# Mamba-2 scan followed by a low-rank mixer: moving the w2 conversions and pair 5's scaling, lending y's banks to pair 3, and pacing the late loads

## The chip, the cores and the metric

One core of one Trainium2 chip runs the whole program. The metric is the device time of one execution in microseconds (us), and the median of several executions where a single number is given. The engines are named as in the profile: PE is the matrix engine (PEld its weight loads), DVE the vector engine, ACT the scalar engine, POOL the general engine, SP the engine that issues the DMAs.

## The reference

Two blocks run one after the other. The first is a chunked state-space scan over 4 batches, 8 heads, 768 positions, head size 32, state size 16, in chunks of 32. The second mixes the first one's output (4 x 768 x 256) along the sequence with a low-rank product and then applies two dense layers.

```
for each chunk c of 32 positions:
    L = exp(cum_i - cum_j) where i >= j, else 0        # cum = cumsum(log a)
    y = ((C B^T) * L) x + (C state) * exp(cum)
    state = exp(sum log a) * state + sum_j B_j x_j exp(cum_end - cum_j)
u  = y + (y^T U V)^T
out = u + relu(u w_ch1) w_ch2
```

U, V, w_ch1 and w_ch2 come as 64-bit floats and are converted to 32 bits on the chip.

## The kernel before, in words

The scan works on *pairs* of 128 positions: `pairs[k]` is batch k // 3 and the (k % 3)-th 256 positions, so there are 12 pairs, k = 0 to 11. "Pair 3" below is k = 3, the first pair of batch 1. Pair k passes these steps, each a function:

- `load_bc(k)` (L111) and `load_x(k)` (L121) issue four loads of B and C and two of x, on SP. All loads of all pairs and all weights stand at the head of SP's program; the stores of the output (L764) come behind them.
- `prep(k)` (L339) scales B and C of the pair by their decays, one DVE instruction (L344) into the tile BC. `decayed(k)` (L351) makes bd from B on POOL (L356).
- `turning(k)` / `turn(k)` (L363) transposes BC on PE into a PSUM bank (tag "w" unless told otherwise), and ACT copies it out: T (L378) and two masked copies Cm (L384).
- `gram(k)` (L398) computes C B^T into four PSUM banks: two of tag "x" and two of tag "z". `mask(k)` (L410) copies them to M with the causal mask, four DVE instructions (L417).
- `state(k)` (L429), on PE, makes each chunk's contribution to the state; `update(k)` (L444) runs the recurrence, three or four DVE instructions (L456, L458), and one POOL instruction (L465) writes Sm.
- `inter(k, 0)`, `intra(k)`, `inter(k, 1)` (L499, L528) are the matmuls of the output, in the two banks of tag "y"; `yout(k)` (L542) copies y out on ACT, and `ytokening(k)` (L551) transposes it back ("tokens").

The first matmul of `inter(k, 1)` waits for whatever instruction was put into `behind["part"]` since `inter(k, 0)`: in the main loop that is the first masking instruction of pair k + 1 on DVE. `apart(copy)` (L469) sets it to a tiny copy instead, which itself waits for the matmuls of `inter(k, 0)`.

There are eight PSUM banks, two for each of the tags w, x, z and y; a tag's banks are handed out in turn, and a bank comes free when its last reader is done.

`to_fp32` (L299) converts one block of 64-bit words in three steps, which other code pulls one at a time: step 1 is two DVE instructions (e, L315, and top, L317) and one on ACT (rest, L319); step 2 is one on ACT (power, L321); step 3 is three on DVE (L323, L325, L327). There are ten blocks in order: U and V together, two eighths and three quarters of w_ch1, and four blocks of w_ch2, called w2 a, b, c and d here. `convert(n)` (L865) runs the next n steps; `convert_ahead()` (L869) runs steps 1 and 2 of the *next* block and then step 3 of the current one.

The dense layers of batch 0 are run plainly. `up` (L701, relu L706 on ACT) fills the first layer in 8 column blocks, m = 0 to 7, each with an x bank and a z bank; `some(2)` runs one m. `down(0)` of batch 0 is two calls of `whole` (L806): two transposes (L810) and then all eight w2 row blocks in order (L816), the last two of which are block d. The other `down` groups (L741) use sums on DVE (L730) and the combined weights `w2s`, made by `operands` (L1010, instructions on L1013).

All engines run in the order in which the code emits (`manual_schedule`), and each engine's queue is strictly in that order. The order around the change is written out by hand: from `mixed()` of batch 0 on it is a list of calls, and from L1028 a loop over k = 3, 4, 5, ... that does prep(k+2), a piece of dense work (`plan`), turning(k+2), inter(k,0), gram(k+1), intra(k), state(k+1), mask(k+1), inter(k,1), yout(k), update(k+1). The `o` tiles that hold the output before its store exist three times.

Of the kernel before, what the change touches and what calls it, by code (L numbers as in the profile page):

```python
# [20 lines left out]
def kernel(  # L21
# [27 lines left out]
    nc = tc.nc  # L49
    P = 128  # L50
# [3 lines left out]
    NPR = NC // 2  # L54
# [8 lines left out]
    H = 64  # L63
# [30 lines left out]
    def fill(n):  # L94
# [10 lines left out]
        in_=a.rearrange("(g b) h (c s) -> g (b h c) s", g=2, s=P).rearrange(  # L105
            "g r s -> r g s"))

    x_sb, bc_sb = {}, {}
    pairs = [(b, q) for b in range(NB) for q in range(NPR)]

    def load_bc(k, blocks=(0, 1)):  # L111
        b, q = pairs[k]
        if k not in bc_sb:
            bc_sb[k] = raw.tile([P, 2, 2, NH, N], FP32, tag="bc", name="bc")
        for c in blocks:
            for i, src in enumerate((B, C)):
                nc.sync.dma_start(  # L117
                    out=bc_sb[k][:, i, c],
                    in_=src[b, :, ts(2 * q + c, P), :].rearrange("h s n -> s h n"))

    def load_x(k, blocks=(0, 1)):  # L121
        b, q = pairs[k]
        if k not in x_sb:
            x_sb[k] = raw.tile([P, 2, NH, D], FP32, tag="x", name="x")
        for c in blocks:
            nc.sync.dma_start(  # L126
                out=x_sb[k][:, c],
                in_=x[b, :, ts(2 * q + c, P), :].rearrange("h s d -> s h d"))


    UV = const.tile([P, 2, NC * RK], FP32)
# [24 lines left out]
    for k in range(NPR):  # L156
# [4 lines left out]
        if k:  # L161
# [4 lines left out]
                      in_=U2.rearrange("(c p) r -> p c r", p=P))  # L166
# [5 lines left out]
    for k in range(2):  # L172
# [3 lines left out]
                                      in_=w13[:, :, ts(k, 2 * P)]))  # L176
# [4 lines left out]
    for m in range(0, NM, 2):  # L181
        load_words(w2[:, m:m + 2],
                   w22[m * P:(m + 2) * P].rearrange("(m p) d -> p m d", p=P))
    for k in range(NPR + 1, NB * NPR):
        load_bc(k)
        load_x(k)


    ident = const.tile([P, P], FP32)
# [54 lines left out]
    for b in range(NB):  # L244
        g, o = divmod(b * NH * NC, R)
# [93 lines left out]
    def prep(k, c=0, n=2):  # L339

        b, q = pairs[k]
        if c == 0:
            st[k] = {"BC": att.tile([P, 2, 2, NH, N], FP32, tag="BC", name="BC")}
        nc.vector.tensor_tensor(  # L344
            out=st[k]["BC"][:, :, c:c + n].rearrange("p i c h n -> p i (c h) n"),
            in0=bc_sb[k][:, :, c:c + n].rearrange("p i c h n -> p i (c h) n"),
            in1=F[:, :, b, 2 * q + c:2 * q + c + n].rearrange("p i c h -> p i (c h)")[
                :, :, :, None].to_broadcast([P, 2, n * NH, N]),
            op=ALU.mult)

    def decayed(k, c=0, n=2):  # L351

        b, q = pairs[k]
        if c == 0:
            st[k]["bd"] = att.tile([P, 2, NH, N], FP32, tag="bd", name="bd")
        nc.gpsimd.tensor_tensor(  # L356
            out=st[k]["bd"][:, c:c + n].rearrange("p c h n -> p (c h) n"),
            in0=bc_sb[k][:, 0, c:c + n].rearrange("p c h n -> p (c h) n"),
            in1=FD[:, b, 2 * q + c:2 * q + c + n].rearrange("p c h -> p (c h)")[
                :, :, None].to_broadcast([P, n * NH, N]),  # L360
            op=ALU.mult)
# [28 lines left out]
    def turn(*args):  # L390
        for _ in turning(*args):
            pass

    def four(tags, *dims):

        return [bank(tags[r], *dims) for r in range(4)]

    def gram(k):  # L398
        s = st[k]
        s["g"] = g = four("xxzz", 2, 2, H)  # L400
        for c in range(2):
            for p in range(2):
                for r in range(4):
                    rows, cols = ts(r, Q), ts(p, H)
                    nc.tensor.matmul(  # L405
                        out=g[r][cols, c], lhsT=s["T"][rows, 0, c, cols],
                        rhs=s["Cm"][rows, :, c, cols], start=(c == 0), stop=True,
                        skip_group_check=True)
# [60 lines left out]
    def apart(copy):  # L469

        behind["part"] = op = copy(out=settled, in_=slot[:, :1])  # L471
        for product in behind.pop("first"):
            tc.add_manual_dep(op.ins, product.ins.name, mybir.DependencyInfo(
                mybir.DependencyClass.Sync, mybir.DependencyReason.DATA))
# [24 lines left out]
    def inter(k, part):  # L499

        b, q = pairs[k]
        s = st[k]
        y = channels(k)
        after = behind.pop("part", None)
        if part == 0:
            after = None
            behind["first"] = []
        for c in range(2):  # L510
            for r in range(4):
                p = (part + r // 2) % 2
                own = st.get(("Sm", b, 4 * q + 2 * c + p))
                if own is not None:
                    product = nc.tensor.matmul(  # L515
                        out=y[p][ts(r % 2, H), r // 2, c], lhsT=own[ts(r, Q)],
                        rhs=s["T"][ts(r, Q), 1, c, ts(p, H)],
                        start=fresh(k, p, range(2 * (r % 2), 2 * (r % 2) + 2)),
                        stop=True, skip_group_check=True)
                    if part == 0:  # L520
                        behind["first"].append(product)
                    if after is not None:
                        tc.add_manual_dep(
                            product.ins, after.ins.name, mybir.DependencyInfo(
                                mybir.DependencyClass.Sync, mybir.DependencyReason.DATA))
                        after = None
# [338 lines left out]
    def convert(n):  # L865
        for _ in range(n):
            next(steps.pop(0))

    def convert_ahead():  # L869

        if len(steps) > 3:
            next(steps.pop(1))
            next(steps.pop(1))
        next(steps.pop(0))
# [5 lines left out]
    def some(n):  # L880
        run(ups[:n])
        del ups[:n]
# [9 lines left out]
        for i in range(2):  # L892
            nc.scalar.copy(out=V4[:, ts(i, HS // 2)], in_=v[i])

    def hold(load, until):

        tc.add_manual_dep(load.ins, until.ins.name, mybir.DependencyInfo(
            mybir.DependencyClass.Sync, mybir.DependencyReason.DATA))

    one, others = slice(0, 1), slice(1, NB)  # L900
    yT[0] = mix.tile([P, NCB, S], FP32, tag="yT", name="yT")
    ytok[0] = mix.tile([P, NC, DM], FP32, tag="ytok", name="ytok")
    project, mixed, ups, plan, downs = mixer(0)
# [74 lines left out]
    keep(others)  # L978
    prep(3)
    decayed(3)  # L980
    convert_ahead()
    some(2)
    convert_ahead()
    some(2)
    turn(3)
    prep(4)
    decayed(4)
    some(2)
    gram(3)
    state(3)  # L990
    mask(3)
    update(3)
    convert_ahead()
    some(2)
    turn(4)
    for pieces in plan[:2]:
        pieces.insert(0, convert_ahead)


    ws = const.tile([P, 5, DF // 2], FP32)  # L1000
# [9 lines left out]
    def operands(n, engine):  # L1010
        for _ in range(min(n, len(work))):
            out, l, r, op = work.pop(0)
            engine.tensor_tensor(out=out, in0=l, in1=r, op=op)  # L1013
# [13 lines left out]
    last = len(pairs)  # L1027
    for k in range(NPR, last + 1):  # L1028
        b, q = divmod(k, NPR)
        pieces = plan[q] if q or b == 1 else []  # L1030
        turns = [turning(k + 2).__next__] * 4 if k + 2 < last else [lambda: None]
        if k > NPR:
            tokens = [ytokening(k - 1).__next__] * 3
            if q == 0:
                late = downs
                project, mixed, ups, plan, downs = mixer(b - 1)
                p4 = late.pop()
                pieces = (late[:1] + tokens + late[1:7] + [project] + late[7:11] + [mixed]
                          + late[11:])
                for at in (-1, -3, -5, -7):  # L1040
                    pieces.insert(at, lambda: operands(1, nc.vector))
                if k == last:
                    run(pieces + list(filled(ups, p4)))
                    break
                pieces += list(filled(plan[0], p4, turns[0], turns[1]))
                turns = turns[2:]
            elif q == 1 and b > 1:
                pieces = list(filled(pieces, tokens[0], turns[0], tokens[1])) + [tokens[2]]
                turns = turns[1:]
            else:  # L1050
                pieces = pieces[:3] + tokens + pieces[3:]
        if k + 2 < last:
            prep(k + 2)
            decayed(k + 2)
        run(pieces + turns)
        inter(k, 0)
        if k + 1 < last:
            gram(k + 1)
        else:
            settle()  # L1060
        intra(k)
        if k + 1 < last:
            state(k + 1)
            mask(k + 1)
        inter(k, 1)
        yout(k)
        if k + 1 < last:
            update(k + 1)
        if q == 1:
            run(plan[3])  # L1070
        if k == NPR + 1:
            operands(4, nc.vector)
    run(downs)

# [29 lines left out]
```

## Time and profile before

| what | value |
|---|---|
| median of 7 executions | 240.03 us (237.79 to 245.09) |
| the profiled execution's own time | 240.46 us |
| its span, first to last instruction | 238.6 us |
| busy over the span | PE 96%, PEld 74%, DVE 65%, ACT 40%, POOL 9% |
| mean granted clock of PE | 0.993 |
| DMA issues: loads of B and C | 48 of 64 KB, of x 24 of 128 KB |
| stores of the output | first issued at 80.9 us |

How to read it: times within the profile are microseconds from the start of the span. A line of the timeline gives start, duration, engine, source line, operation, what it writes and reads, the shape, the count of like instructions merged, and in brackets how long the engine had been idle before it and what ended that. A busy PE is not a PE at full speed, since the ends of matmuls are modelled; the granted clock is shown apart, as a share of full speed.

### The profile page before, as it was taken

To read this page: it belongs to the slowest core of one execution; us is meant where nothing else is said; L and a number is where in the kernel's file an instruction comes from. 1 tells how busy PE (TensorE), PEld (TensorE's weight loads), DVE (VectorE), ACT (ScalarE), POOL (GpSimd) and SP (SyncE) were. 2 spreads that over 40 slices of the span, in tenths; PEclk is the share of its full clock that TensorE was granted. 3 is DMA by queue.
4 is the path that set the end of the run, shared out by engine and by line. 5 is a ranking of instruction groups with operands and counts; after the bars stand their busy time and mean duration, and the time that the engine had idled before them with its cause. 6 is when DMAs were issued, how large, how long until landed. Compare 5 with 4: busy or idle time off the path is not lost.

```text
span 238.6 us, 7374 instructions
## 1 busy us (share of the span) xinstructions
PE 229.2 (96%) x3166; PEld 176.2 (74%) x3166; DVE 155.2 (65%) x363; ACT 95.6 (40%) x245; POOL 20.6 (9%) x40
## 2 busy tenths in 40 slices
PE   7988899799999999999999999999999999999995
PEld 5666566456688988565799987565799896559994
DVE  3676898799996666475896661556974372478511
ACT  5344646837514212537614112466312014663110
POOL 4221001120330300002021100010000000000000
PEclk9999999979999999999999999999999999999999
DMA  6975969798888810100001010000001011000111
GB/s 82 116 89 155 280 83 337 100 118 102 102 112 112 134 44 0 44 3 3 3 3 47 5 44 27 21 3 0 3 3 47 14 33 44 0 0 3 44 47 45
DMA packets 81909, 14.60 MB, mean 61 GB/s; under 512 B 76052, under 2 KB 80084, under 8 KB 81876
## 3 DMA queue, kind: packets, MB, share of 16 engines
q1 hardware_dynamic: 81876, 14.13, 32.4%
q8 instruction: 25, 0.41, 0.8%
q14 instruction: 8, 0.07, 0.1%
HBM read 10.98 MB, written 3.15 MB: 59 GB/s over the span
## 4 chain that ended last, share of the span: by engine, by line
PE 79%; SPq 10%; DMA 4%; DVE 3%; ACT 2%; issue 1%; DVEq 0%; ACTq 0%
PE x L741 17%; PE x L633 14%; PE z L741 13%; PE z L633 10%; SPq L117 7%; PE y L537 3%; PE x L816 3%; PE y L515 3%; DMA words<-in_moe_w_ch_dram 3%; PE x L405 2%; PE x L701 2%; SPq L126 2%; PE w L586 2%; PE w L557 2%; PE z L701 2%; PE w L438 2%
## 5 line engine op out<-in xcount | busy, mean ns | idle before, releaser
L633 PE MATMUL x<-t,ws 128*128 128x384 f32 x72 | 28.6, 495 | 0.0
L741 PE MATMUL x<-w2s,words 128*128 128x128 f32 x176 | 23.2, 275 | 0.0
L741 PEld LDWEIGHTS x<-w2s,words 128*128 128x128 f32 x176 | 21.6, 193 | 0.0
L621 ACT ACTIVATE gT<-gT 128x384 f32<-128x384 f32 x36 | 19.0, 528 | 2.4 <-DVE gT L642 2.3
L465 POOL TENSOR_TENSOR Sm<-S,slot 128x256 f32<-128x256 f32 (+1 forms) x12 | 8.8, 736 | 120.7 <-DVE S L458 86.1
L633 PEld LDWEIGHTS x<-t,ws 128*128 128x128 f32 x72 | 12.5, 190 | 8.0 <-ACT top L638 1.3
L730 DVE TENSOR_TENSOR words<-gT 128x512 f32<-128x512 f32 (+1 forms) x28 | 16.7, 596 | 0.6 <-ACT gT L621 0.6
L642 DVE TENSOR_TENSOR gT<-z,top 128x384 f32<-128x384 f32 x12 | 6.7, 558 | 15.2 <-PE z L633 13.4
L417 DVE TENSOR_TENSOR M<-x,causal 128x256 int32<-128x256 int32 x24 | 9.1, 420 | 9.3 <-PE z L405 8.0
L638 ACT COPY e<-x 128x384 f32<-128x384 f32 x12 | 5.8, 479 | 23.1 <-PE x L633 19.7
L799 ACT COPY o<-x 128x128 f32<-128x128 f32 x11 | 2.9, 266 | 28.6 <-PE x L741 28.6
L549 ACT COPY yT<-y 128x256 f32<-128x256 f32 x24 | 7.8, 375 | 15.4 <-PE y L515 15.4
L405 PE MATMUL x<-Cm,T 32*64 32x128 f32 x192 | 12.1, 291 | 1.7 <-ACT Cm L384 1.5
L701 PE MATMUL x<-yT,w 128*128 128x384 f32 x32 | 13.1, 534 | 0.6 <-DVE yT L601 0.6
L458 DVE SCALAR_TENSOR_TENSOR S<-S,kept,w 128x64 f32<-128x64 f32 x40 | 11.2, 279 | 2.3 <-PE w L438 0.5
L741 PE MATMUL x<-w,gT 128*128 128x128 f32 x88 | 12.6, 285 | 0.0
L676 DVE TENSOR_SCALAR gT<-x 128x384 f32<-128x384 f32 x12 | 6.7, 557 | 9.1 <-PE x L633 9.1
L741 PEld LDWEIGHTS x<-w,gT 128*128 128x128 f32 x88 | 10.8, 191 | 2.3 <-issue 1.6
L356 POOL TENSOR_TENSOR bd<-bc,FD 128x256 f32<-128x256 f32 (+1 forms) x13 | 9.4, 722 | 30.6 <-ACT FD L282 19.1
L741 PE MATMUL z<-w2s,words 128*128 128x128 f32 x88 | 11.9, 278 | 0.0
L515 PE MATMUL y<-T,Sm 32*64 32x64 f32 x352 | 11.0, 230 | 0.7 <-ACT settled L471 0.4
L701 PE MATMUL z<-yT,w 128*128 128x384 f32 x32 | 11.6, 486 | 0.0
(179 smaller groups left out, 507.0 us busy)
## 6 DMA issues: line engine op xcount, KB each, us to landing
words<-in_moe_w_ch_dram SPq DMA_DIRECT2D x7, 512.0 KB, 7.2
x<-in_x_dram SPq DMA_DIRECT2D x24, 128.0 KB, 3.3
out_dram<-o SPq DMA_DIRECT2D x11, 256.0 KB, 2.1
bc<-in_B_dram SPq DMA_DIRECT2D x24, 64.0 KB, 3.5
bc<-in_C_dram SPq DMA_DIRECT2D x24, 64.0 KB, 3.0
words<-in_moe_w_ch_dram SPq DMA_DIRECT2D x2, 256.0 KB, 3.3
words<-in_moe_V_dram SPq DMA_DIRECT2D x1, 192.0 KB
words<-in_moe_U_dram SPq DMA_DIRECT2D x1, 192.0 KB, 4.9
```

The costliest lines, as they stand in the source:

```text
L117: nc.sync.dma_start(out=bc_sb[k][:, i, c], in_=src[b, :, ts(2 * q + c, P), :].rearrange("h s n -> s h n"))
L356: nc.gpsimd.tensor_tensor(out=st[k]["bd"][:, c:c + n].rearrange("p c h n -> p (c h) n"), in0=bc_sb[k][:, 0, c:c + n].rearrange("p c h n -> ...
L405: nc.tensor.matmul(out=g[r][cols, c], lhsT=s["T"][rows, 0, c, cols], rhs=s["Cm"][rows, :, c, cols], start=(c == 0), stop=True, skip_group_ ...
L417: done = nc.vector.tensor_tensor(out=M[:, r].bitcast(INT32).rearrange("p c s i -> p (c s) i"), in0=g[r].bitcast(INT32).rearrange("p c s i ...
L458: done = nc.vector.scalar_tensor_tensor(out=new, in0=st["S", b], scalar=kept[:, b, j, None], in1=add, op0=ALU.mult, op1=ALU.add)
L465: nc.gpsimd.tensor_tensor(out=s["Sm"][:, sl], in0=s["S"][:, sl].rearrange("p i (s d) -> p i s d", s=2), in1=slot[:, None, :, None].to_broa ...
L515: product = nc.tensor.matmul(out=y[p][ts(r % 2, H), r // 2, c], lhsT=own[ts(r, Q)], rhs=s["T"][ts(r, Q), 1, c, ts(p, H)], start=fresh(k, p ...
L621: nc.scalar.activation(g, g, AF.Relu)
L633: nc.tensor.matmul(out=X[name], lhsT=lhsT[:, ts(i, P)], rhs=rhs, start=start, stop=True, skip_group_check=True)
L701: nc.tensor.matmul(out=g, lhsT=w1[:, n, ts(m, P)], rhs=uT[:, n, ts(k, HS)], start=(n == 0), stop=(n == NCB - 1))
L730: nc.vector.tensor_tensor(out=S[v][:, lo:hi], in0=l[:, lo:hi], in1=r[:, lo:hi], op=op)
L741: nc.tensor.matmul(out=X[name], lhsT=lhsT[:, i], rhs=rhs[:, i], start=start and u is None and i == 0, stop=True, skip_group_check=True)
```

## The change

- The list of loads from pair 4 on: from pair 7 on, each load of B, C or x waits until the load two before it has landed.
- `gram` takes the tags of its banks; pair 3's goes into one x bank, one z bank and both y banks. `turn(4)` uses a y bank in place of a w bank.
- The conversions of w2: a's steps 1 and 2 come one m later in the list; b's come after m = 4; step 3 of b comes after update(3) and pair 5's scaling; c's steps 1 and 2 come in the loop at k = 3 after inter(3, 0), step 3 of c with steps 1 and 2 of d at k = 4 after inter(4, 0), and step 3 of d after update(5), ahead of the four w2s operands.
- prep(5) and decayed(5) move from the head of k = 3 to right behind update(3).
- `apart` on ACT is added behind inter(3, 0) and inter(4, 0).

```diff
+    def hold(load, until):
+        tc.add_manual_dep(load.ins, until.ins.name, mybir.DependencyInfo(
+            mybir.DependencyClass.Sync, mybir.DependencyReason.DATA))
...
     for k in range(NPR + 1, NB * NPR):
+        del paced[:-2]
         load_bc(k)
         load_x(k)
+        if k > NPR + 3:
+            for i in range(2, len(paced)):
+                hold(paced[i], paced[i - 2])
...
-    def gram(k):
+    def gram(k, tags="xxzz"):
         s = st[k]
-        s["g"] = g = four("xxzz", 2, 2, H)
+        s["g"] = g = four(tags, 2, 2, H)
...
     prep(3)
     decayed(3)
-    convert_ahead()
     some(2)
     convert_ahead()
     some(2)
     turn(3)
+    some(2)
+    convert_ahead()
     prep(4)
     decayed(4)
-    some(2)
-    gram(3)
+    gram(3, "xzyy")
     state(3)
     mask(3)
     update(3)
-    convert_ahead()
+    prep(5)
+    decayed(5)
+    convert(1)
     some(2)
-    turn(4)
-    for pieces in plan[:2]:
-        pieces.insert(0, convert_ahead)
+    turn(4, 0, 2, "y")
...
-        if k + 2 < last:
+        if NPR + 2 < k + 2 < last:
             prep(k + 2)
             decayed(k + 2)
         run(pieces + turns)
         inter(k, 0)
+        if k < NPR + 2:
+            apart(nc.scalar.copy)
+            (convert_ahead if k > NPR else lambda: convert(2))()
         if k + 1 < last:
             gram(k + 1)
...
         if k == NPR + 1:
+            convert(1)
             operands(4, nc.vector)
```

`paced` collects the load instructions in the order in which they are issued; NPR is 3, NB is 4, and `some(2)` is one m of the first dense layer.

More of the change, by code (lines that the diff above doesn't have):

```diff
@@ L106 @@
             "g r s -> r g s"))
-    x_sb, bc_sb = {}, {}
+    x_sb, bc_sb, paced = {}, {}, []
     pairs = [(b, q) for b in range(NB) for q in range(NPR)]
+    def hold(load, until):
+        tc.add_manual_dep(load.ins, until.ins.name, mybir.DependencyInfo(
+            mybir.DependencyClass.Sync, mybir.DependencyReason.DATA))
     def load_bc(k, blocks=(0, 1)):
@@ L116, in load_bc @@
             for i, src in enumerate((B, C)):
-                nc.sync.dma_start(
+                paced.append(nc.sync.dma_start(
                     out=bc_sb[k][:, i, c],
-                    in_=src[b, :, ts(2 * q + c, P), :].rearrange("h s n -> s h n"))
+                    in_=src[b, :, ts(2 * q + c, P), :].rearrange("h s n -> s h n")))
     def load_x(k, blocks=(0, 1)):
@@ L125, in load_x @@
         for c in blocks:
-            nc.sync.dma_start(
+            paced.append(nc.sync.dma_start(
                 out=x_sb[k][:, c],
-                in_=x[b, :, ts(2 * q + c, P), :].rearrange("h s d -> s h d"))
+                in_=x[b, :, ts(2 * q + c, P), :].rearrange("h s d -> s h d")))
     UV = const.tile([P, 2, NC * RK], FP32)
@@ L893, in spread @@
             nc.scalar.copy(out=V4[:, ts(i, HS // 2)], in_=v[i])
-    def hold(load, until):
-        tc.add_manual_dep(load.ins, until.ins.name, mybir.DependencyInfo(
-            mybir.DependencyClass.Sync, mybir.DependencyReason.DATA))
     one, others = slice(0, 1), slice(1, NB)
```

## The prediction

> **What bounds the kernel now.** I read the page's busy shares first, then where DVE and PE stand idle, then the granted clock, then the rows of single operations. All times are us in the one profiled execution.
>
> ```profile
> PE 229.2 (96%) x3166; PEld 176.2 (74%) x3166; DVE 155.2 (65%) x363; ACT 95.6 (40%) x245; POOL 20.6 (9%) x40
> ...
> DVE  3676898799996666475896661556974372478511
> ```
>
> PE is full as an average, so only a stage in which PE stands or runs slowly can give time. The third line is DVE in 40 slices of 6 us: the ninth to twelfth slices (48 to 72 us) show 9. There DVE is as full as PE. The change touches 39 to 70 us, so its worth is read there.
>
> Next, the windows view: length, busy time of PE, PEld, DVE, ACT and POOL, then the granted clock.
>
> ```profile
> 26.85:30.27 3.42, 2.31 (x42) 1.27 (x32) 2.94 (x9) 2.30 (x7) 0.00 (x0) 1.00 1.02 281
> 43.92:47.33 3.41, 1.93 (x22) 0.80 (x28) 1.78 (x4) 3.41 (x9) 0.62 (x1) 1.00 0.79 97
> 47.33:50.75 3.42, 3.42 (x61) 2.03 (x52) 2.99 (x10) 0.31 (x1) 0.00 (x0) 0.50 1.03 109
> 44.63:65.96 21.33, 19.35 (x410) 12.63 (x410) 18.09 (x39) 12.95 (x30) 4.07 (x5) 0.92 0.94 111
> ```
>
> From 47.33 to 50.75 PE ran at half clock, after 3.4 us in which it was busy for only 1.93. A stretch with 2.31 busy, higher up, was not followed by a drop. The last line is the stage from the end of m = 4 to the start of whole(0).
>
> The timeline of PE shows the pause, its releaser and the end of the stage:
>
> ```profile
> 43.44 1.45 PE L701 MATMUL z<-yT,w 128*128 128x384 f32 x4
> 46.38 0.70 PE L405 MATMUL x<-Cm,T 32*64 32x128 f32 x3 [1.48 <-ACT Cm L384]
> ...
> 65.89 0.44 PE L810 MATMUL x<-ident,yT 128*128 128x128 f32 x2
> 66.16 3.62 PE L816 MATMUL x<-w,gT 128*128 128x256 f32 x16
> ```
>
> gram(3) (L405) waited for ACT. ACT's timeline shows T3 and Cm3 late, though turn(3) ended on PE at 42.0: two conversions and m = 3's relus are queued ahead of them.
>
> ```profile
> 44.99 0.59 ACT L378 COPY T<-w 128x512 f32<-128x512 f32 x1
> 45.46 0.86 ACT L384 ACTIVATE Cm<-w,slot 128x256 f32<-128x256 f32 x2
> ```
>
> DVE in the same stage; idle time is in brackets:
>
> ```profile
> 47.21 0.69 DVE L344 TENSOR_TENSOR BC<-bc,F 128x512 f32<-128x512 f32 x1 [1.60 <-DMA bc<-in_C_dram]
> ...
> 54.09 0.68 DVE L344 TENSOR_TENSOR BC<-bc,F 128x512 f32<-128x512 f32 x1
> ...
> 61.00 1.10 DVE L323 SCALAR_TENSOR_TENSOR rest<-top,rest 128x512 f32<-128x512 f32 x1
> 62.02 1.11 DVE L325 SCALAR_TENSOR_TENSOR power<-words,power 128x512 int32<-128x512 int32 x1
> 63.16 0.69 DVE L327 SCALAR_TENSOR_TENSOR w<-rest,power 128x512 f32<-128x512 f32 x1
> 64.03 0.75 DVE L417 TENSOR_TENSOR M<-x,causal 128x256 int32<-128x256 int32 x2 [0.17 <-PE z L405]
> ```
>
> DVE starts the stage at 47.21, when pair 4's C lands (prep(4)), and then stands only 1.25 us in all until 73.42. The two rows of 1.1 are 0.42 longer than the like rows alone (0.69), and POOL's rows lie over them:
>
> ```profile
> 60.56 0.99 POOL L465 TENSOR_TENSOR Sm<-S,slot 128x256 f32<-128x256 f32 x1 [8.27 <-DVE S L458]
> 61.51 1.07 POOL L356 TENSOR_TENSOR bd<-bc,FD 128x256 f32<-128x256 f32 x1
> ```
>
> **The change on PE alone.** ACT: w2 a's words arrive at 40.32 as before, its two instructions end by 41.52, m = 3's relus (0.37 apart, the second behind PE's 41.53) by 42.3, then T3 and Cm3 (0.59, 0.86) by 43.6 in place of 46.3. So gram(3) starts when m = 4 ends, at 44.63. With one x, one z and two y banks it waits for no relu of m = 4 (y's banks were last read by ACT at 38); at pair 5's pace (63.43 to 63.98) it takes 0.55 in place of 1.77. state(3) 0.4, m = 5 2.58: PE is at 48.2. turn(4) now needs a y bank, so the third masking instruction of pair 3: DVE's prep(4) at 47.21, then 0.60, two masks of 0.33, and the third's 0.42 give 48.9. That is a new PE wait of 0.75, less than the gap that was followed by the drop. turn(4) 0.44, m = 6 2.58, turn(5) 0.44 (its BC5 is ready by 51.9 to 52.3, below), inter 0.32, gram(4) 0.58, intra 0.79, state 0.42, inter(3,1) 0.38: 54.9. m = 7 waits for pair 4's first mask (55.2), 2.58 to 57.8; tokens and turn(6) 0.88, inter 0.31, gram(5) 0.55, intra 0.79, state 0.29, inter 0.39: PE reaches whole(0) at 61.05, against 65.96. PE alone would gain 4.9: the pause and the half clock (1.48 and 3.42 x 0.5 = 1.71), and the waits for banks.
>
> **The same on DVE.** No DVE instruction is taken away; five DVE pieces of conversion lie behind prep(4) before and after. The order is new: after update(3), at 50.3, stands prep(5), which needs pair 5's last load.
>
> ```profile
> 48.29 0.58 SPq L117 DMA_DIRECT2D bc<-in_C_dram  x1
> ```
>
> ```profile
> bc<-in_C_dram SPq DMA_DIRECT2D x1, 64.0 KB, 2.7
> ```
>
> It is issued at 48.29 and lands 2.7 later (the second fence, that issue alone); with the 0.17 that pair 4's took from landing to the operation, prep(5) starts at 51.16. DVE stands 0.86. This is new: before, prep(5) ran at 54.09 with no wait. Everything behind it on DVE is delayed with it: step 3 of w2 b, masks and update of pair 4, prep(6), c, masks and update of pair 5, and at the end step 3 of d, by start-to-start rows: prep 0.60 twice; step 3 1.93 three times (41.00 to 42.93) and 0.08 for the last one's own end; e and top 0.67 twice; four masks 1.33 twice; updates 1.23 and 0.83. Sum 13.13. POOL's overlaps: bd5 once 0.42 (Sm3 falls into the new wait), Sm4 and bd6 0.84, Sm5 and bd7 0.84: 2.10. Step 3 of d ends at 51.16 + 13.13 + 2.10 = 66.4.
>
> whole(0) starts behind pair 5's first mask: d's 2.85 with POOL, update(5)'s 0.83 and three masks of 0.33 less one overlap lie between, so at 61.9. It reaches the seventh w2 block, d's first, after 0.37 + 6/8 of 3.46, at 64.8. Before, d was done at 63.85, before whole(0) began. Now PE stands 1.6 until 66.45. Before, it was at this block at 65.96 + 0.37 + 2.60 = 68.93. Gain: **2.48**, half of PE's 4.9. From there PE's rows are dense to p1 (76.74), and the lead is kept: DVE's four operands 2.5, prep(7) 0.6, four sums 2.5 and a difference 0.5 end at 72.5, so pair 6's first mask is done at 72.9 and inter(5,1) comes at 76.35 - 2.48 = 73.9.
>
> **What I cost at nothing.** The two apart copies are 0.19 of ACT each; at 54.0 and 60.3 they follow T5/Cm5 and T6/Cm6, and inter(k,1) comes at 54.5 and 60.7. Without that cover each costs up to 0.2; against it, inter(k,1) no longer waits for DVE's mask, and from both sides I take 0. ACT's rest and power of c and d, 1.2 each, stand ahead of yout(3) and yout(4), whose readers come 1.4 or more later. decayed(5) keeps its place on POOL between Sm3 and bd6. The pacing adds waits to 30 loads on SP, no byte. Landings in that stretch are 2.4 to 4.1 (median 3.3), so two in flight make a pair of loads per 3.3 and a pair of the scan per 9.9 from 56.2 on (pair 6's x: 53.22 + 3.0). Pair 7's C is there at 62.8 and read at 68.9; pair 8's at 72.7 (76.7 at 4.1 each), wanted at about 75.2, where DVE has a 2.24 gap soon after. Queued behind them on SP are the stores: the first goes at about 103 in place of 80.92, and the fourth output tile, which needs the first one's store, is written at 124.6. Without that cover it costs PE the difference. It might also give back waits that the profile calls issue (0.36 and 0.14 on PE in the stage), or lose as much; I take 0, since DVE sets the end there.
>
> **Sum.** On the profiled execution 240.46 - 2.48 = 237.98. It lies 0.43 above the median of those shown (240.03), so the median is **237.6**.
>
> **Two rules weighed.** The Trainium skill's page "SBUF — State Buffer", section "Who interferes with whom", says that between DVE and GpSimd the later one is blocked for the whole of the other's instruction. The rows show 0.42 for each overlap with instructions of 0.99 and 1.07; by the rule as a full block of about 1.0 each, the five overlaps would come to an estimated 5 and no gain would be left, and I go by the rows. Its page "TensorE: Matmul & The Clock Gate", section "HAM oscillation — how this bites in real kernels", warns only of PE gaps above some 3.4 us. By that the new gap of 1.6 costs nothing; here the clock halved after a gap of 1.48, so rival B is kept.
>
> **The rivals.**
>
> *A, the forecast* (0.50): DVE sets the end at d's last step; 237.6, its own range 236.8 to 238.4.
>
> *B, the clock* (0.23): PE's 1.6 at the seventh block is longer than the 1.48 after which the clock halved for 3.42. For it: that row. Against: there gram(3) was also sparse, 1.93 busy in 3.41, and with 2.31 nothing happened; 1.6 idle in an otherwise dense stretch leaves 1.8 only if both ends fall into the same 3.4. Price 1.71: 239.3.
>
> *C, DVE is lighter* (0.19): POOL's overlaps cost between 0 and 2.1, if its instructions fall beside other work. At 0, d is ready at 64.3, PE stands 0.3, and the gain is 4.6 (235.4); at half it is 3.5, so 236.5. Against: the same POOL instructions follow the same updates, with two-input DVE work behind them.
>
> *D, slower* (0.08): prep(5) heads DVE's queue and pair 5's last load lands late. Each us is a us of the end; the gain is gone when it lands 5.2 after issue in place of 2.7. The longest landing of a B or C load is 8.3: 243.2. Against: its neighbours' rows are 3.1 and 3.5.
>
> **How the numbers follow.** The range: below, C a little past its half, 236.2; above, B with the load at 3.5 in place of 2.7, 239.3 + 0.8, and 0.2 of rounding: 240.3. Faster by over 1% (about what a measurement of this kernel can tell from no change) means below 237.6: half of A and all of C, 0.44. Within 1%: the other half of A, all of B, a quarter of D: 0.50. Slower: 0.06.
>
> **What would show it.** Right: gram(3) at about 44.6 with no half clock behind it; turn(4) behind a mask; prep(5) waiting for a DMA; PE idle within whole(0) until d's L327. Wrong: no wait within whole(0) (C), a granted clock of 0.50 behind it (B), prep(5) past 53 (D), or stores that hold up an output tile.

## The result, and the profile after

The changed kernel takes 237.83 us (median of 27 executions, 235.83 to 241.53), the kernel before 240.01 (64). The ratio is 0.9911, 95% interval 0.9893 to 0.9928: 2.1 us less. Medians are over all executions, while the ratios and their intervals leave out the slow ones, which lie over 1.5% above the fastest of the same kernel. The profiled execution took 238.28 with a span of 236.4. Lines of the changed file stand 4 to 9 further down than before.

The page, busy shares and DVE's 40 slices:

```profile
PE 226.7 (96%) x3166; PEld 175.0 (74%) x3166; DVE 154.1 (65%) x363; ACT 96.2 (41%) x247; POOL 20.1 (8%) x40
...
DVE  3575799778998575566997472556964362478411
```

The averages say nothing: the same work, in a span 2.2 us shorter. The stage shows it. The windows view of the changed kernel (length, busy time of PE, PEld, DVE, ACT and POOL with the count of instructions, granted clock, DMA share, GB/s): 3.4 us from 45.15, just behind the first matmul of gram(3), and from there to whole(0).

```profile
45.15:48.57 3.42, 3.42 (x72) 2.23 (x73) 2.18 (x7) 2.16 (x4) 0.62 (x1) 1.00 1.10 134
45.15:63.07 17.92, 15.96 (x408) 11.09 (x408) 14.23 (x35) 12.57 (x28) 3.62 (x5) 1.00 0.80 95
```

The pause before gram(3) and the half clock are not there. From the start of m = 4's z rows to whole(0) it takes 19.4 (43.69 to 63.07), where it took 22.5 (43.44 to 65.89). PE's timeline shows the border and the places where PE now stands:

```profile
43.69 1.45 PE L710 MATMUL z<-yT,w 128*128 128x384 f32 x4
45.08 0.32 PE L414 MATMUL x<-Cm,T 32*64 32x128 f32 x1
...
55.60 0.42 PE L447 MATMUL w<-x,bd 64*32 64x64 f32 x21 [1.33 <-issue]
61.94 0.51 PE L546 MATMUL y<-M,x 64*32 64x64 f32 x34 [0.62 <-issue]
63.07 0.44 PE L819 MATMUL x<-ident,yT 128*128 128x128 f32 x2
63.35 2.76 PE L825 MATMUL x<-w,gT 128*128 128x256 f32 x12
66.46 1.13 PE L825 MATMUL x<-w,gT 128*128 128x256 f32 x4 [0.36 <-DVE w L336]
```

The last row is the stand of PE inside whole(0): PE waits there for DVE's last instruction of w2 d. Two pauses with no releaser, 1.33 in state(4) and 0.62 in intra(4), are new in size. DVE:

```profile
46.33 0.69 DVE L353 TENSOR_TENSOR BC<-bc,F 128x512 f32<-128x512 f32 x1 [1.15 <-DMA bc<-in_C_dram]
...
50.77 0.73 DVE L353 TENSOR_TENSOR BC<-bc,F 128x512 f32<-128x512 f32 x1 [1.26 <-DMA bc<-in_C_dram]
...
56.10 1.31 DVE L467 SCALAR_TENSOR_TENSOR S<-S,kept,w 128x64 f32<-128x64 f32 x4 [0.67 <-PE w L447]
...
65.41 0.99 DVE L336 SCALAR_TENSOR_TENSOR w<-rest,power 128x512 f32<-128x512 f32 x1
```

prep(5) waits for its load, and d is ready at 66.40. A second profile of the same kernel (e5 below) has no issue pause in this stage, and is the cleaner picture:

```profile
51.89 0.63 PE L383 MATMUL w<-ident,BC 128*128 128x128 f32 x4 [0.17 <-DVE BC L353]
61.33 0.44 PE L819 MATMUL x<-ident,yT 128*128 128x128 f32 x2 [0.46 <-DVE M L426]
61.61 2.75 PE L825 MATMUL x<-w,gT 128*128 128x256 f32 x12
65.69 1.13 PE L825 MATMUL x<-w,gT 128*128 128x256 f32 x4 [1.32 <-DVE w L336]
```

whole(0) waits 0.46 for pair 5's mask and then stands 1.32 for w2 d. Both are waits for DVE.

One number is used for all kernels below: the *stage*, from the start of prep(4) on DVE, which is when its load is there, to the first matmul of p1, the group of dense-layer matmuls that follows (L741, now L750). Both starts are read from the timelines.

| kernel | prep(4) | p1 | stage |
|---|---|---|---|
| before | 47.21 | 76.67 | 29.46 |
| changed, two profiles | 46.33, 45.66 | 74.52, 73.75 | 28.19, 28.09 |
| e8: before + pacing | 46.28 | 75.37 | 29.09 |
| e4: before + filled pause | 46.36 | 76.05 | 29.69 |

Behind p1 nothing moved: 238.6 - 76.67 = 161.9 us remain before, 236.4 - 74.52 = 161.9 after. The stage gives 1.3 or 1.4 against the profile before, and 0.9 or 1.0 against e8's, in which that kernel had no half clock. In the changed kernel's profiles prep(4) also began 0.9 and 1.5 sooner than in the one of before, but e8 and e4, which are the kernel before up to there, began it at 46.3 as well. So single profiles scatter by that much, and what makes up the rest of the 2.1 stays open.

The half clock in the profile before is not the usual case. One drop of 3.42 makes the mean granted clock 0.993, as in that profile; of the 107 executions of the kernel before that were timed beside the experiments, 70 had 0.997 or more, which leaves no room for it. Such executions still differ: on the chip of e5 their medians are 238.97 (21 executions of the kernel before) and 237.51 (7 of the changed one), 1.5 less. So most of the gain cannot be this half clock avoided. e8's profile shows how the kernel before looks without it:

```profile
45.29 0.70 PE L414 MATMUL x<-Cm,T 32*64 32x128 f32 x3 [0.69 <-ACT Cm L393]
```

There the pause ahead of gram(3) is 0.69, the clock stays at 1.00, and the stage is 0.37 shorter than with 1.48 and the half clock.

### The profile page after: what moved, and what is told of

Its sections match the earlier page's. It is cut to its first block, busy times and chain, and to the rows that moved or that the text cites. A ratio compares the mean times of both kernels' runs of the same rounds, so it can differ in the third digit from the quotient of the medians.

```text
span 236.4 us, 7378 instructions
## 1 busy us (share of the span) xinstructions
PE 226.7 (96%) x3166; PEld 175.0 (74%) x3166; DVE 154.1 (65%) x363; ACT 96.2 (41%) x247; POOL 20.1 (8%) x40
## 4 chain that ended last, share of the span: by engine, by line
PE 91%; DVE 4%; issue 2%; ACT 1%; POOL 0%; DVEq 0%; POOLq 0%; ACTq 0%
PE x L750 17%; PE x L642 14%; PE z L750 13%; PE z L642 10%; PE x L710 5%; PE z L710 4%; PE y L546 4%; PE y L524 3%; PE x L414 3%; PE x L825 2%; PE w L566 2%; PE w L595 2%; PE w L383 2%; PE w L447 2%; PE x L82 2%
## 5 line engine op out<-in xcount | busy, mean ns | idle before, releaser
L750 PE MATMUL x<-w2s,words 128*128 128x128 f32 x176 | 23.2, 275 | 0.0
L750 PEld LDWEIGHTS x<-w2s,words 128*128 128x128 f32 x176 | 21.6, 193 | 0.0
L750 PE MATMUL x<-w,gT 128*128 128x128 f32 x88 | 12.6, 285 | 0.0
L710 PE MATMUL x<-yT,w 128*128 128x384 f32 x32 | 12.0, 496 | 0.6 <-DVE yT L610 0.6
L750 PEld LDWEIGHTS x<-w,gT 128*128 128x128 f32 x88 | 10.8, 191 | 2.3 <-issue 1.6
L750 PE MATMUL z<-w2s,words 128*128 128x128 f32 x88 | 11.9, 278 | 0.0
L546 PE MATMUL y<-M,x 64*32 64x64 f32 x768 | 10.7, 224 | 1.1 <-issue 1.1
L353 DVE TENSOR_TENSOR BC<-bc,F 128x512 f32<-128x512 f32 (+1 forms) x15 | 9.0, 609 | 4.1 <-DMA bc<-in_C_dram 2.4
```

What stands on the lines that cost most here:

```text
L353: nc.vector.tensor_tensor(out=st[k]["BC"][:, :, c:c + n].rearrange("p i c h n -> p i (c h) n"), in0=bc_sb[k][:, :, c:c + n].rearrange("p i ...
L546: nc.tensor.matmul(out=y[p][ts(i, Q), n, c], lhsT=x_sb[k][half, c, h], rhs=s["M"][half, h // 2, c, h % 2], start=fresh(k, p, [i]), stop=Tr ...
L710: nc.tensor.matmul(out=g, lhsT=w1[:, n, ts(m, P)], rhs=uT[:, n, ts(k, HS)], start=(n == 0), stop=(n == NCB - 1))
L750: nc.tensor.matmul(out=X[name], lhsT=lhsT[:, i], rhs=rhs[:, i], start=start and u is None and i == 0, stop=True, skip_group_check=True)
```

## The experiments

Each was timed beside the kernel before on the same chip; the intervals are 0.5 to 1.0% wide, so times tell little between 0.991 and 0.996, and the verdicts rest on the profiles. In the profiles of e3, e9 and e12 the clock was at half for a time before 30 us, in e6's between 32 and 36. There the stage begins late (47.9 to 49.5), when the loads of pairs 4 and 5 have landed, and DVE waits for neither. Neither their spans nor their stages compare with the others, as e12's rows of prep(4) and prep(5) show:

```profile
49.50 0.69 DVE L353 TENSOR_TENSOR BC<-bc,F 128x512 f32<-128x512 f32 x1
...
52.59 0.68 DVE L353 TENSOR_TENSOR BC<-bc,F 128x512 f32<-128x512 f32 x1
```

**e5, the changed kernel again.** 

> The changed kernel itself, beside the kernel before on the chip of the next three. Every theory: 0.991 of the kernel before, as in the result; it is the measure for the other three. Its profile tells which of the waits come again: PE's pause in state(4) near 1.3 at the same matmul, a stand in whole(0) between 0.3 and 1.6, and DVE's wait of about 1 before pair 5's scaling.

Measured: 237.57 us, 0.9925 (0.9891 to 0.9959). The pauses put down to issue did not come again, which was not expected: 1.95 in the stage in one profile of this kernel and none in the other. DVE's wait for pair 5's load was 2.20, and the stand in whole(0) 1.32.

**e3, more work on DVE ahead of d.**

```diff
         if k == NPR + 1:
+            for _ in range(2):
+                nc.vector.tensor_tensor(out=ws[:, 0], in0=A[2], in1=A[3], op=ALU.add)
             convert(1)
```

> The changed kernel with two more DVE instructions of the operands' kind (about 0.6 to 1.0 each beside POOL) ahead of step 3 of w2 d; they write a tile that is written again later. Theory (d's step 3 sets when whole(0) can end): the stand in whole(0) grows from 0.4 to between 1.6 and 2.0 and the time by 1.2 to 1.6, to about 239.2. Rival (DVE has slack there, PE sets the end): at most 0.3 more.

Measured: 241.95 us, 1.0002 (0.996 to 1.0044), 0.8 to 0.9% above the changed kernel's ratios, or about 2 us where 1.2 to 1.6 were forecast. PE's row at the seventh w2 block:

```profile
69.59 1.13 PE L825 MATMUL x<-w,gT 128*128 128x256 f32 x4 [2.36 <-DVE w L336]
```

The stand is 2.36, against 0.36 and 1.32 in the changed kernel: what is put on DVE there arrives at PE, and DVE sets this place. How much of the growth is the two instructions' cannot be read from a stage that began late.

**e7, without d's last step.**

```diff
+    nc.gpsimd.memset(w2[:, NM - 2:], 0.0)
...
         if k == NPR + 1:
-            convert(1)
             operands(4, nc.vector)
```

> The changed kernel without step 3 of w2 d: its three DVE instructions are left out, and block d is set to zero early by POOL instead, so this part of w_ch2 is missing from the output. Theory (d's step 3 sets the end of whole(0)): no stand in whole(0); the time falls by that stand, 0.4 to 0.8, to 0.988 of the kernel before, and no further, since PE with its issue pauses is next. If PE had no pauses it would be up to 2. Rival (PE sets the end, DVE has slack): no change.

Measured: 236.85 us, 0.9913 (0.9881 to 0.9945).

```profile
61.56 0.44 PE L819 MATMUL x<-ident,yT 128*128 128x128 f32 x2 [0.44 <-DVE M L426]
61.84 3.62 PE L825 MATMUL x<-w,gT 128*128 128x256 f32 x16
```

whole(0) still starts behind the mask, but its sixteen matmuls run through. The stage is 26.27, 1.8 to 1.9 under the changed kernel's. Against e5, 1.6 of it is the stand with the start behind it: the first call of whole takes 3.73 (61.56 to 65.29) where it took 5.33 (61.33 to 66.66). The span was 234.3 against e5's 235.7. The time does not show it: the ratios differ by 0.001, or 0.3 us, well within their intervals.

**e12, d ahead of update(5).**

```diff
+        if k == NPR + 1:
+            convert(1)
         if k + 1 < last:
             update(k + 1)
...
         if k == NPR + 1:
-            convert(1)
             operands(4, nc.vector)
```

> The changed kernel with step 3 of w2 d ahead of update(5) on DVE, not behind it; nothing is left out. Theory (what lies between pair 5's masks and d's last instruction sets the stand in whole(0): update(5)'s 0.83, d's 1.93 and POOL's overlaps of 0.6 to 0.8, which start only with update(5)): d ends 1.4 to 1.7 sooner, the stand in whole(0) is gone or under 0.2, and the time falls by that stand, 0.4 to 1.3: 0.987 to 0.990 of the kernel before. Pair 5's state comes 1.9 later, at about 66, and is read at 69. Rival (update(5) late holds up inter(5, 0) or pair 6's C B^T, or PE's issue pauses use up the gain): 0.991 to 0.9925 or more.

Measured: 239.53 us, 0.9938 (0.9888 to 0.9987).

```profile
65.13 3.62 PE L825 MATMUL x<-w,gT 128*128 128x256 f32 x16
...
76.23 0.32 PE L447 MATMUL w<-x,bd 64*32 64x64 f32 x9 [1.00 <-issue]
```

The stand is gone as forecast; a pause of 1.00 fell behind it. The stage of 27.37 cannot be set against the changed kernel's, because DVE had no wait for pair 5's load here (1.26 and 2.20 there). The time shows no gain, so the rival is not excluded.

**e2, conversion ahead of pair 5's scaling.**

```diff
     update(3)
+    convert(1)
     prep(5)
     decayed(5)
-    convert(1)
```

> The changed kernel with step 3 of w2 b ahead of pair 5's scaling, so that DVE works while that load is under way. Theory (the 1.26 us wait before pair 5's scaling is on DVE's path to the end): the wait falls under 0.2, d's last instruction ends 0.9 to 1.2 earlier, and PE's stand in whole(0) (about 0.4) is gone; the time falls by only 0.4 to 0.6, to about 237.3, because PE with its issue pauses is then the later of the two. If the pauses are short in this kernel, up to 1.2 (236.6). Rival (that wait is hidden): no change, 237.8.

Measured: 239.73 us, 0.9955 (0.9909 to 1.0002). The theory failed in its second half: DVE no longer waits for the load, but POOL's instructions now lie over the conversion, prep(5) starts 5.75 after prep(4) (4.44 and 5.39 in the changed kernel), and PE waits for it.

```profile
52.64 0.99 DVE L336 SCALAR_TENSOR_TENSOR w<-rest,power 128x512 f32<-128x512 f32 x1
53.55 0.68 DVE L353 TENSOR_TENSOR BC<-bc,F 128x512 f32<-128x512 f32 x1
```

```profile
54.38 0.63 PE L383 MATMUL w<-ident,BC 128*128 128x128 f32 x4 [1.59 <-DVE BC L353]
...
67.31 1.13 PE L825 MATMUL x<-w,gT 128*128 128x256 f32 x4 [0.98 <-DVE w L336]
```

turning(5) stands 1.59 and the masks behind it wait for PE in turn; the stand in whole(0), forecast to go, is 0.98. The stage, 27.64, is about 0.5 shorter; the time does not show it, and single stages scatter by more (e11 below).

**e9, a smaller piece in that wait.**

```diff
     update(3)
+    next(steps.pop(1))
     prep(5)
     decayed(5)
     convert(1)
...
-            (convert_ahead if k > NPR else lambda: convert(2))()
+            (convert_ahead if k > NPR else lambda: convert(1))()
```

> The changed kernel with step 1 of w2 c (two short DVE instructions, 0.67 together, and one on ACT) ahead of pair 5's scaling, where DVE waits for that pair's load (1.26 to 2.20 in the changed kernel's two profiles), and not after inter(3, 0). Theory (from that wait on DVE's queue sets the end): the wait shrinks by about 0.67, pair 5's scaling is not later, and from pair 4's scaling to d's first block in whole(0) it takes 19.4 in place of 20.0 to 20.1; the time falls by 0.6, to 0.989 of the kernel before. Rival (the load's landing or PE sets the end): 20.0 again and 0.991 to 0.9925.

Measured: 239.06 us, 0.9939 (0.9903 to 0.9976); stage 28.19. The rival's 20.0 came (48.00 to 67.97), but it was not put to the test. The wait for pair 5's load was gone, as it was in e3 and e12, which lack this edit: the stage began late (48.00) and the load had landed. prep(5) took 1.10 under POOL, DVE then waited 0.68 for gram(4) and 0.56 for state(4), and PE 0.36 for DVE in whole(0). So each waits for the other in turn, by some half a microsecond.

**e4, the pause of the kernel before filled.**

```diff
     some(2)
+    warm(7, "y")
     gram(3)
```

> The kernel before, with 1.5 us of idle matmuls into a free y bank in the pause ahead of gram(3), so that the clock has no reason to drop. Theory (DVE was nearly full behind that pause, with 1.1 us of idle time in all up to 66.6): the granted clock stays at 1.0, but the time falls by at most 0.9 to 1.1, to about 239.0. Rival (the half clock alone was the loss): all of 1.7 comes back, 238.3. Second rival (the pause does not cause the drop): the clock still halves, no change.

Measured: 239.49 us, 0.9946 (0.9915 to 0.9976), or 1.3 us, from 0.6 to 2.0. The windows over the place where the clock had been at half:

```profile
43.90:47.30 3.40, 3.40 (x40) 1.76 (x39) 1.94 (x3) 3.32 (x9) 0.62 (x1) 1.00 0.93 119
47.30:50.70 3.40, 3.32 (x47) 2.06 (x43) 3.12 (x10) 0.35 (x1) 0.58 (x1) 1.00 0.99 106
```

The clock stays up in this profile. That does not rule out the second rival, since the kernel before mostly runs without the drop too. Between 1.0 and 1.7 the interval does not decide. Most of the 1.3 is not a half clock avoided either: among the executions with a clock of 0.997 or more the medians are 239.16 (9) and 240.30 (23 of the kernel before), 1.1 apart. The stage does not show the gain: it is 29.69 with a pause of 0.93 in state(4), against 29.46. What the filled pause gained stays open.

**e8, pacing alone, and e1, everything but the pacing** (the `hold` loop added to the kernel before, and taken out of the changed one).

> The kernel before with the pacing of the loads from pair 7 on, and nothing else of the change. Theory (the pacing is free, and gives nothing): 0.998 to 1.002 of the kernel before. Rival (the pacing is worth part of the gain, since fewer loads are under way beside PE's own fetches and the stores): 0.995 to 0.997, with shorter issue pauses from 57 us on.

> The changed kernel without the pacing of the loads. Theory (DVE's queue sets the end of the stage; the pacing is free): the time stays within 0.5 us of the changed kernel's 237.8, d's last DVE instruction ends near 66.4 again, and PE's two pauses put down to issue (1.33 in state(4), 0.62 in intra(4)) are about as long, since the first of them lies ahead of the first paced load. Rival (the pacing is what gained, by keeping PE's pauses short): 1 to 2 us longer, with more or longer issue pauses from 57 us on.

Measured: e8 239.75 us, 1.002 (0.9988 to 1.0051); e1 239.62 us, 0.9952 (0.991 to 0.9993). e8 gains nothing, as the theory has it. e1's median is higher than the changed kernel's, but the intervals overlap, so the 0.5 us of the theory is neither shown nor excluded. The profile holds something else: PE's pause, and the windows behind it.

```profile
57.19 0.42 PE L444 MATMUL w<-x,bd 64*32 64x64 f32 x21 [1.51 <-issue]
57.92 2.43 PE L707 MATMUL x<-yT,w 128*128 128x384 f32 x4
```

```profile
58.00:59.00 1.00, 1.00 (x3) 0.57 (x4) 0.84 (x4) 0.65 (x2) 0.00 (x0) 0.73 1.01 132
59.00:60.00 1.00, 1.00 (x3) 0.53 (x2) 1.00 (x3) 0.00 (x0) 0.92 (x1) 0.50 1.02 95
...
61.00:62.00 1.00, 1.00 (x3) 0.48 (x3) 1.00 (x3) 0.00 (x0) 0.00 (x0) 0.56 0.75 97
```

After a pause of 1.51 PE was at half clock again; with 0.73 and 0.56 in the windows at its ends it lasted from about 58.5 to 61.9. This is rival B's mechanism, at another pause than the one named. That stage is 29.13. Six of e1's twelve executions had a clock of 0.997 or more; their median is 238.0 against 240.30, so the lower clock of the other six goes with its higher median. Whether the pacing makes such pauses rarer was not settled: the first paced load is issued near the pause, and pauses come and go in one and the same kernel.

**e6, the instruction stream shifted by 80.**

```diff
     project()
+    small = bank("y", Q)
+    for i in range(20):
+        rows = ts(i % 4, Q)
+        nc.tensor.matmul(out=small[rows], lhsT=ident[rows, rows], rhs=ident[rows, rows],
+                         start=True, stop=True, skip_group_check=True)
     mixed()
```

> The changed kernel with 20 tiny matmuls (40 matmul records and 40 weight loads) ahead of mixed(), where PE waits anyway; nothing else differs, but PE's later instructions lie 80 further on in its stream. Theory (the pauses put down to issue are PE waiting for its own instructions: a block of 256 comes by a transfer of 16 KB, and a block that holds only the small matmuls of gram and intra is used up before the next one is there): the pause of 1.33 leaves state(4), the new border lies in intra(3) behind a block with m = 6 in it, and both pauses fall under 0.3; PE is at whole(0) 1.2 to 1.9 sooner, DVE's waits for PE (0.67 and 0.18) go, d's last instruction ends 0.8 sooner, and the time falls by about 0.8, to 0.988 of the kernel before. Rival (the pauses come from the loads' traffic or from that place in the program): 1.3 again in state(4), no change of time.

Measured: 239.05 us, 0.9989 (0.9962 to 1.0015): no gain over the kernel before, a miss, and not one of the clock alone: with 0.997 or more the medians are 238.73 (7) and 238.97 (21). The pauses left state(4) and intra(4), but a longer one came inside the tiny matmuls themselves, and the clock fell behind it:

```profile
30.73 0.39 PE L975 MATMUL y<-ident 32*32 32x32 f32 x22 [2.59 <-issue]
```

Since e5 has no pause in state(4) either, their absence alone proves nothing, and the theory is not tested by this run.

**e10, the old banks for gram(3) and turn(4), and e11, no apart copies.**

```diff
-    gram(3, "xzyy")
+    gram(3)
...
-    turn(4, 0, 2, "y")
+    turn(4)
```

```diff
         if k < NPR + 2:
-            apart(nc.scalar.copy)
             (convert_ahead if k > NPR else lambda: convert(2))()
```

> The changed kernel with pair 3's C B^T in two x and two z banks and turn(4) in a w bank, as before. Theory (these banks help PE, and PE is not the later one): gram(3) waits for m = 4's second relu, about 0.7, m = 5 then for pair 3's masks, some 1 to 1.5 more, and turn(4) for update(3); PE loses about 1 to 2 of its lead over DVE, the stand in whole(0) shrinks by as much, and the time rises by 0 to 0.5: 0.992 to 0.994 of the kernel before. Rival (the banks are what gained): 0.996 or more.

> The changed kernel without the two added apart copies, so that inter(3, 1) and inter(4, 1) wait for the first mask of the next pair on DVE, as before. Theory: both come after that mask anyway, within 0.3; no change, 0.991 to 0.9925 of the kernel before. Rival (DVE's lateness reaches PE through this wait): inter(4, 1) or inter(3, 1) stands 0.5 or more, and the time rises by up to that.

Measured: e10 239.53 us, 0.995 (0.9905 to 0.9994), stage 27.87; e11 238.72 us, 0.9924 (0.9889 to 0.996), stage 27.34. In e10 gram(3) waits 0.21 for a relu, whole(0) starts at 61.70, and the stand is 0.86: whole(0) starts 15.9 behind prep(4), against 15.7 in e5, so the banks' help to PE was over-rated (1 to 2 were expected). The ratio lies between the theory's range and the rival's, and its interval holds both. e11 stands nowhere for the missing copies, as expected. Both only take something away, and yet their stages are 0.2 to 0.9 shorter than the changed kernel's: that is how far single stages scatter.

## Why the prediction held, point by point

*The pause and the clock.* gram(3) was to start at 44.63, when m = 4 ends, with no drop behind. It started at 45.08 and 44.76 in the two profiles, behind m = 4, with a clock of 1.00. But the loss of 4.9 on PE, 1.71 of it for the half clock, was worked out from one execution, and most do not have that drop. The start of the seventh block at 68.93, from which the gain was counted, holds it too. That this did little harm is luck: in e8, without the half clock, the stage of the kernel before was only 0.37 shorter.

*DVE sets the end.* This was the heart of it, and is shown by e3, e7 and e5: PE, even without pauses, stands in whole(0) until DVE has w2 d ready, and without that step it does not stand. From prep(5)'s start to d's end 15.24 were forecast (51.16 to 66.4); measured are 14.58 in e5 (51.05 to 65.63) and 15.63 in the first profile (50.77 to 66.40).

*POOL's overlaps*, 2.10 in the sum, were over-rated. In e5 the rows that are longer than alone are e and top of d (0.84 against 0.42), power and w of d (0.99 against 0.69): 1.4. That explains the 0.66 that e5 is under the forecast. The range's rival C had this direction, but not to its half. Rival B did not come: PE stood 0.36 and 1.32 at d, and in e3 2.36, and the clock stayed at 1.00 behind it.

*The pauses put down to issue* were taken as 0, and this is the term that missed. They were 1.95 in the first profile, where whole(0) started at 63.07 and not at the forecast 61.9; DVE waited 0.67 and 0.18 for PE through them. That d still ended at 66.40, as forecast, is luck: 0.66 less for POOL and a prep(5) 0.39 earlier nearly cancel 0.85 more for PE's pauses. The stand, forecast at 1.6, was 0.36 in that profile and 1.32 in e5.

*prep(5)'s wait* was forecast at 0.86: 1.26 and 2.20. It is not pure loss, since DVE was early: prep(5) started at 50.77 and 51.05, where 51.16 was forecast.

*The new wait of turn(4)* (0.75) came as 0.88 in e1 and 0.55 in e2, and not at all in the changed kernel's two profiles.

*Costed at nothing:* the apart copies (e11) and the pacing (e8) cost nothing that can be seen. The last of the paced loads are issued at 95.0 and the first store at 96.0, where 103 was estimated, well before an output tile is wanted again.

```profile
94.96 0.99 SPq L131 DMA_DIRECT2D x<-in_x_dram  x2
96.00 1.64 SPq L773 DMA_DIRECT2D out_dram<-o  x3
```

*The size.* 2.48 was forecast against one profile, which held a half clock; 2.1 (1.7 to 2.6 by the interval) was measured. The stages of the profiles show 0.9 to 1.4 of it, so the time confirms the size, and the working behind it is confirmed only in part.

## What to carry to other kernels

Where two engines are both nearly full, work out both queues through the stage and take the later one at each meeting point; the gain of a wait removed on one is what the other's queue leaves of it, by the forecast here half. Once both are nearly level, moving a piece between places shifts the wait from one to the other (e2). Before a single profile is believed to a tenth of the effect, take a second one of the same kernel, and look in the list of all executions whether what it shows, here the half clock, is the usual case.

## What the runs showed of the hardware

*PE may be waiting for its own instructions; these rows suggest it, and no run shows it.* Pauses with no releaser sit at the same matmul in several kernels: 21 rows of state(4) follow the pause in the changed kernel (1.33), e1 (1.51), e8 (0.28), e9 (0.55) and e11 (0.70). In e2, e3, e5, e7, e10 and e12 there is none at that place. In e4, where four matmul records stand ahead, 25 follow it:

```profile
58.43 0.56 PE L438 MATMUL w<-x,bd 64*32 64x64 f32 x25 [0.93 <-issue]
```

So the place seems to go with the position in PE's stream. The changed kernel's page has an instruction queue (packets, MB, share of the DMA engines):

```profile
q8 instruction: 25, 0.41, 0.7%
```

That is 25 packets of some 16 KB. If all are PE's, which the page does not say, they are about 253 for each of them, from its 6,332 matmuls and loads. The Trainium skill's page "Runtime: NRT & Kernel Launch", section "Instruction fetch mechanics", gives blocks of 16 KiB with 256 instructions, which agrees; it calls the crossing mostly hidden, and here the pauses without a releaser are up to 1.51 in state(4). Why the same kernel pauses 1.33 once and not at all the next time stays open.

*The half clock does not follow the length of a pause alone.* It came for 3.42 after 1.48 (before), for 3.4 after 1.51 (e1) and again behind the 2.59 of e6, not after 1.33 and not after the 2.36 of e3, where PE was busy for 1.23 of the 3.4 from 66.0 on. The skill's page "TensorE: Matmul & The Clock Gate", section "What's actually happening", has a window of 3.4 us that runs freely: the length of the drop agrees. Its section "HAM oscillation — how this bites in real kernels" warns of gaps above 3.4 us; here the clock halved behind 1.48 and 1.51. That the phase of the window decides was not tried.
